# Two steps of a feed-forward at a time: elementwise instructions over pairs of tiles in double PSUM banks

## The chip, the cores and the metric

The kernel runs on one core of a Trainium2 chip (trn2). The metric is the device time of one execution in microseconds, and a kernel's number is the median of its runs. Five engines work side by side and wait for each other through semaphores: PE (TensorE, matrix products, with its weight loads PEld), DVE (VectorE), ACT (ScalarE), POOL (GpSimd) and SP, which issues the DMAs. Each engine takes its instructions strictly in the order in which they were written; an instruction that waits holds up everything behind it on its engine.

## What is computed

The input is `x`, four batches of 12416 tokens with 128 channels, and 32 inducing points. First comes an attention of the inducing points over the tokens, then one of the tokens over its result; the outcome goes, token by token, through a gated feed-forward with 1536 hidden channels:

```python
def mab(q, kv):
    s = scale * (q @ kv.transpose(0, 2, 1))
    s = s - s.max(-1, keepdims=True)
    a = np.exp(s)
    a /= a.sum(-1, keepdims=True) + 1e-09
    return a @ kv
h = mab(I, x)            # (4, 32, 128)
x = mab(x, h)            # (4 * 12416, 128)
g = x @ w_gate
out = (g * (1 / (1 + np.exp(-g))) * (x @ w_val)) @ w_out
```

All of it is float32. Products whose operands are split into a leading part and a rest (`hi` and `lo`, type fp32r) are summed so that the result keeps float32's accuracy.

## The kernel before

**Tiles and columns.** The tokens of a batch are cut into 25 columns of 512 or 480 tokens (`COLS`; in each batch 13 columns of 512, then 12 of 480). A column runs through 12 tiles (`NT`), one for each 128 hidden channels. One (column, tile) is a slot; a batch has 300 of them. The weights of the tokens' attention and of the gate and value projections are multiplied together beforehand (`st.w`, tile `tw`), so that a slot's gate and value are one product each of a stacked attention matrix (`stack`) with a piece of `tw`.

**A slot.** `front` (L680) issues the products g (L691) and v (L692), each into a single PSUM bank of the six of pool `ps_gv`. `gate` (L695) runs silu on ACT from g's bank into `silu` (two buffers). `value` (L699) multiplies v by it on DVE: into `h`, a pool of three buffers (`BF[1]`), or, for the tiles in `DVE_TILES` (1, 5 and 9), back into v's own PSUM bank. `split` (L707), called one slot later, makes `h_hi` by a cast on ACT (L713; on DVE for tile 11 and for slots with a burst, below) and `h_lo = h - h_hi` (L715) on POOL, or on DVE for `DVE_TILES`, whose h lies in PSUM. `back` (L719) adds three products into the bank o of the column: `wo_lo` by hi (L729), `wo_hi` by hi (L730), `wo_hi` by lo (L731). After tile 11 `evac` copies o out on DVE (L738) and SP stores it. The 12 slots of the very first column (`u.whole`) have a simpler form and lie in the start-up.

**The order of the work.** All instructions are written out by the loop at L769 to L794. In each slot it writes front, gate and value, then the split of the slot before, then steps of the attention of this batch and of the next one that are due (`plan`, `post`), then as many backs as keep no more than `ahead` slots between front and back. `ahead` is `SKEW` (5) as a rule, so the three products into o come five slots behind their g and v. Ahead of a burst it climbs by one in `RAMP` slots, up to `HI` (10), and falls back to `SKEW` at the burst: the stored backs are then written at once. A burst is a slot in which ACT runs exponentials of the next batch (`exp1_part` L302, `exp2` L456); there are two for each of the batches that follow, and one (`E0`) in the first. The attention's own products (L270, L318, L420) take banks of `ps_gv` and `ps_o`; on DVE its steps are copies, transposes and reductions of around 0.6 us, on POOL they are subtractions and products (L453, L467, L483).

**Buffers.** An instruction that writes a buffer waits until all who read its last content are done. For `h` these are the cast on ACT and the subtraction on POOL, three h-tiles back. For `h_hi` (11 buffers) and `h_lo` (10) it is the products into o.

Of the kernel before, what the change touches and what calls it, by code (L numbers as in the profile page):

```python
# [105 lines left out]
def induced_set_attention_then_swiglu(ctx: ExitStack, tc: tile.TileContext, xt, xn, ind, wgv, wo, out):  # L106
# [573 lines left out]
    def front(st, b, c, t):  # L680
# [11 lines left out]
        nc.tensor.matmul(out=u.v[:, :n], lhsT=st.w[:, wcol(1, t)], rhs=rhs, start=True, stop=True)  # L692
        return u

    def gate(u):  # L695
        u.s = sip.tile([P, WF], F32, name="silu")
        nc.scalar.activation(out=u.s[:, :u.n], in_=u.g[:, :u.n], func=AF.Silu)  # L697

    def value(u):  # L699
        n = u.n  # L700
        if u.whole:
            u.h = hip.tile([P, WB], F32, name="h_hi")[:, :WF]
        else:
            u.h = u.v if u.t in DVE_TILES else hp.tile([P, WF], F32, name="h")
        nc.vector.tensor_mul(out=u.h[:, :n], in0=u.v[:, :n], in1=u.s[:, :n])  # L705

    def split(u):  # L707
        if u.whole:
            return
        n = u.n  # L710
        u.hi = hip.tile([P, WB], F32R, name="h_hi")[:, u.at[1]:u.at[1] + WF]
        u.lo = lop.tile([P, WB], F32R, name="h_lo")[:, u.at[2]:u.at[2] + WF]
        (nc.vector.tensor_copy if u.cast_dve else nc.scalar.copy)(out=u.hi[:, :n], in_=u.h[:, :n])  # L713
        eng = nc.vector if u.t in DVE_TILES or u.last else nc.gpsimd
        eng.tensor_sub(out=u.lo[:, :n], in0=u.h[:, :n], in1=u.hi[:, :n].bitcast(F32))  # L715

    acc = {}

    def back(u):  # L719
# [4 lines left out]
        ws = slice(P * t, P * t + P)
        if u.whole:
            k = t % (WP // P)
            nc.tensor.matmul(out=o[:, :n], lhsT=pieces[f"o{t // (WP // P)}"].w[:, P * k:P * k + P], rhs=u.h[:, :n], start=(t == 0), stop=(t == NT - 1))  # L727
        else:
            nc.tensor.matmul(out=o[:, :n], lhsT=wo_lo[:, ws], rhs=u.hi[:, :n], start=(t == 0), stop=False)  # L729
            nc.tensor.matmul(out=o[:, :n], lhsT=wo_hi[:, ws], rhs=u.hi[:, :n], start=False, stop=False)  # L730
            nc.tensor.matmul(out=o[:, :n], lhsT=wo_hi[:, ws], rhs=u.lo[:, :n], start=False, stop=(t == NT - 1))  # L731
# [23 lines left out]
    ahead = len(pend)
    for b in range(B):
        nxt = attention(b + 1, (one, oneb)[(b + 1) % 2]) if b + 1 < B else None
        if nxt is not None:
            nxt.steps = plan(nxt, PA if b == 0 else PB)
            if b == 0:  # L760
                cur.steps.append((nxt.e1, lambda: run(f"e2:52:{NTB}")))
                for q in range(2, NF):
# [4 lines left out]
        bursts = (nxt.bursts if nxt is not None else set()) | ({E0} if b == 0 else set())
        last_burst = max(bursts, default=0)
        for slot in range(NT if b == 0 else 0, SLOTS):  # L769
            c, t = slot // NT, slot % NT  # L770
            u = front(cur, b, c, t)
            gate(u)
            value(u)
            u.cast_dve = t in CAST
            u.last = b == B - 1 and slot == SLOTS - 1
# [4 lines left out]
            if slot in bursts:  # L780
                u.cast_dve = True
                split(u)
                pend.append(wait.pop(0))
            for a in (cur, nxt):
                while a is not None and a.steps and a.steps[0][0] <= slot:

                    if pend and pend[0].t in getattr(a.steps[0][1], "acc", ()):
                        break
                    a.steps.pop(0)[1]()
            ahead = min(ahead + 1 / RAMP, HI) if nxt is not None and slot < last_burst else max(ahead - 1 / RAMP, SKEW)  # L790
            if slot in bursts:
                ahead = SKEW - (b == 0)
            while len(pend) + len(wait) > ahead:
                back(pend.pop(0))  # L794
# [44 lines left out]
```

## Time and profile before

| | |
|---|---|
| three runs | 1454.93 us median (1454.5 to 1455.03) |
| profiled execution, span of its instructions | 1453.1 us |
| PE busy | 1441.8 us, 99% |
| DVE, ACT, POOL busy | 1187.8, 1281.9, 1207.9 us (82%, 88%, 83%) |
| PE in two quiet stretches (1160 to 1260 us, 1300 to 1400 us) | 100.00 of 100 us in each |

The span is that of one profiled execution. Busy time of an engine is the time in which at least one of its instructions ran; neighbours overlap a little, so mean durations added up come to more than busy time. In a timeline row the first number is the start in us, the second the length, and a bracket at the end tells how long the engine had been idle and what ended that. In a group's row stand the count, the busy us, the mean ns of one, and the idle time before them.

### The profile page before, as it was taken

Reading aid. Unit: us, or ns where it says so; the run is one execution under the profiler, and the core shown is the slowest. Engines: PE = TensorE matmul, PEld = TensorE weight load, DVE = VectorE, ACT = ScalarE, POOL = GpSimd, SP = SyncE. Lnnn points to the kernel's source line nnn. Section 1 sums busy time; section 2 is a strip of 40 time slices with the busy share of each in tenths; the row PEclk is TensorE's granted clock in tenths of the full one; section 3 lists DMA queues with packets and bytes.
Section 4 is the critical chain, followed back from the end, with each engine's and each line's share of the span. In section 5 each row is a group of like instructions: output and inputs, shape, how many; then the busy total and the mean of one; then the engine's idle time right before and its main releaser. Section 6 shows DMA issues by size and latency. Waiting matters only on the chain.

```text
span 1453.1 us, 24926 instructions
## 1 busy us (share of the span) xinstructions
PE 1441.8 (99%) x7452; PEld 1173.5 (81%) x7452; DVE 1187.8 (82%) x2080; ACT 1281.9 (88%) x2388; POOL 1207.9 (83%) x995
## 2 busy tenths in 40 slices
PE   8999999999999999999999999999999999999999
PEld 5577788788887787888888778688888888888887
DVE  6888778887888788888788778988888878878877
ACT  5888898799998887999999888799999999999997
POOL 1689778888998778898899878879889889889987
PEclk9999999999999999999999999999999999999999
DMA  9233522321143242211123522321111111111110
GB/s 369 68 98 126 185 74 97 106 64 56 36 138 136 88 137 106 70 52 42 35 69 111 189 78 93 107 79 35 42 36 42 37 44 37 40 40 38 39 41 21
DMA packets 50822, 119.80 MB, mean 82 GB/s; under 512 B 11392, under 2 KB 28288, under 8 KB 50688
## 3 DMA queue, kind: packets, MB, share of 16 engines
q1 hardware_dynamic: 50688, 118.22, 24.9%
q8 instruction: 59, 0.97, 0.3%
q14 instruction: 75, 0.61, 0.1%
HBM read 62.87 MB, written 25.43 MB: 61 GB/s over the span
## 4 chain that ended last, share of the span: by engine, by line
PE 95%; DMA 2%; ACT 1%; POOL 1%; DVE 0%; SPq 0%; issue 0%; DVEq 0%; ACTq 0%; POOLq 0%
PE gv L691 18%; PE o L729 18%; PE gv L692 18%; PE o L730 18%; PE o L731 18%; PE gv L270 2%; PE o L318 1%; DMA s_all<-wgv 1%; DMA xt<-xt 1%; PE o L270 1%; PE o L727 1%; POOL h_lo L715 0%; ACT silu L697 0%; PE gv L420 0%; ACT h_hi L713 0%; PE gv L398 0%
## 5 line engine op out<-in xcount | busy, mean ns | idle before, releaser
L715 POOL TENSOR_TENSOR h_lo<-h,h_hi 128x512 fp32r<-128x512 f32 (+1 forms) x890 | 1110.9, 1273 | 198.4 <-ACT h_hi L713 140.4
L697 ACT ACTIVATE silu<-gv 128x512 f32<-128x512 f32 (+1 forms) x1200 | 704.7, 588 | 109.3 <-PE gv L691 76.3
L705 DVE TENSOR_TENSOR h<-gv,silu 128x512 f32<-128x512 f32 (+1 forms) x891 | 594.5, 668 | 199.0 <-ACT silu L697 147.7
L713 ACT CAST h_hi<-h 128x512 fp32r<-128x512 f32 (+1 forms) x788 | 474.7, 602 | 30.1 <-DVE h L705 25.3
L691 PE MATMUL gv<-stack,tw 128*128 128x512 f32 (+1 forms) x1200 | 465.9, 388 | 2.1 <-DVE stack L543 1.3
L692 PE MATMUL gv<-stack,tw 128*128 128x512 f32 (+1 forms) x1200 | 461.5, 385 | 0.7 <-ACT silu L697 0.4
L729 PE MATMUL o<-h_hi,wo_lo 128*128 128x512 f32 (+1 forms) x1188 | 458.4, 386 | 0.0
L730 PE MATMUL o<-h_hi,wo_hi 128*128 128x512 f32 (+1 forms) x1188 | 456.9, 385 | 0.0
L731 PE MATMUL o<-h_lo,wo_hi 128*128 128x512 f32 (+1 forms) x1188 | 456.3, 384 | 0.0
L691 PEld LDWEIGHTS gv<-stack,tw 128*128 128x128 f32 x1200 | 225.4, 188 | 50.5 <-ACT tw L412 2.6
L729 PEld LDWEIGHTS o<-h_hi,wo_lo 128*128 128x128 f32 x1188 | 223.0, 188 | 51.8 <-issue 12.1
L692 PEld LDWEIGHTS gv<-stack,tw 128*128 128x128 f32 x1200 | 224.9, 187 | 47.8 <-ACT silu L697 4.2
L731 PEld LDWEIGHTS o<-h_lo,wo_hi 128*128 128x128 f32 x1188 | 222.6, 187 | 40.5 <-POOL h_lo L715 0.4
L730 PEld LDWEIGHTS o<-h_hi,wo_hi 128*128 128x128 f32 x1188 | 223.1, 188 | 38.9
L705 DVE TENSOR_TENSOR gv<-gv,silu 128x512 f32<-128x512 f32 (+1 forms) x297 | 201.8, 680 | 40.2 <-ACT silu L697 39.1
L715 DVE TENSOR_TENSOR h_lo<-gv,h_hi 128x512 fp32r<-128x512 f32 (+1 forms) x297 | 197.3, 664 | 0.9
L713 ACT CAST h_hi<-gv 128x512 fp32r<-128x512 f32 (+1 forms) x294 | 167.5, 570 | 4.9 <-DVE gv L705 3.9
L738 DVE COPY ob<-o 128x512 f32<-128x512 f32 (+1 forms) x100 | 66.3, 663 | 0.8 <-PE o L731 0.8
L713 DVE CAST h_hi<-h 128x512 fp32r<-128x512 f32 (+1 forms) x103 | 52.0, 506 | 0.0
L483 POOL TENSOR_TENSOR a_lo<-aT,a_hi 128x480 fp32r<-128x480 f32 (+2 forms) x26 | 34.6, 1330 | 0.0
L190 POOL TENSOR_TENSOR wgv_sb<-s_all 128x512 int32<-128x512 int32 x2 | 2.9, 1455 | 28.9 <-ACT s_all L178 28.9
L467 POOL TENSOR_TENSOR s_all<-s_all,sm 128x512 f32<-128x512 f32 (+2 forms) x27 | 26.1, 967 | 0.0
(155 smaller groups left out, 476.2 us busy)
## 6 DMA issues: line engine op xcount, KB each, us to landing
xt_sb<-xt SPq DMA_DIRECT2D x32, 896.0 KB, 5.2
xn_sb<-xn SPq DMA_DIRECT2D x18, 896.0 KB, 5.6
out<-ob SPq DMA_DIRECT2D x52, 256.0 KB, 2.0
out<-ob SPq DMA_DIRECT2D x48, 240.0 KB, 2.0
stack<-a_hi SPq DMA_DIRECT2D x96, 64.0 KB, 2.0
stack<-a_lo SPq DMA_DIRECT2D x96, 64.0 KB, 2.0
stack<-a_hi SPq DMA_DIRECT2D x96, 60.0 KB, 2.0
stack<-a_lo SPq DMA_DIRECT2D x96, 60.0 KB, 2.0
```

The source lines that it names most:

```text
L270: nc.tensor.matmul(out=ps[32 * j:32 * j + 32, 32 * (lo - b0):32 * (hi - b0)], lhsT=lhsT, rhs=st.xt[q][:, lo - CH0[q]:hi - CH0[q], j, :], s ...
L483: eng.tensor_sub(out=st.al[q][:, :n], in0=st.at[q][:, :n], in1=st.ah[q][:, :n].bitcast(F32))
L691: nc.tensor.matmul(out=u.g[:, :n], lhsT=st.w[:, wcol(0, t)], rhs=rhs, start=True, stop=True)
L692: nc.tensor.matmul(out=u.v[:, :n], lhsT=st.w[:, wcol(1, t)], rhs=rhs, start=True, stop=True)
L697: nc.scalar.activation(out=u.s[:, :u.n], in_=u.g[:, :u.n], func=AF.Silu)
L705: nc.vector.tensor_mul(out=u.h[:, :n], in0=u.v[:, :n], in1=u.s[:, :n])
L713: (nc.vector.tensor_copy if u.cast_dve else nc.scalar.copy)(out=u.hi[:, :n], in_=u.h[:, :n])
L715: eng.tensor_sub(out=u.lo[:, :n], in0=u.h[:, :n], in1=u.hi[:, :n].bitcast(F32))
L729: nc.tensor.matmul(out=o[:, :n], lhsT=wo_lo[:, ws], rhs=u.hi[:, :n], start=(t == 0), stop=False)
L730: nc.tensor.matmul(out=o[:, :n], lhsT=wo_hi[:, ws], rhs=u.hi[:, :n], start=False, stop=False)
L731: nc.tensor.matmul(out=o[:, :n], lhsT=wo_hi[:, ws], rhs=u.lo[:, :n], start=False, stop=(t == NT - 1))
L738: nc.vector.tensor_copy(out=ob[:, :n], in_=o[:, :n])
```

## The change

Everything behind the start-up works on pairs of slots of one column: tiles 0 and 1, 2 and 3, and so on to 10 and 11.

- The six single banks become three double banks (`ps_two`, 2 x 512 columns each). `fronts` writes the products in the order g g v v, the g's into the halves of one double bank and the v's into those of another.
- Silu, the product with v, the cast and the subtraction each become one instruction over 2 x 512 (or 2 x 480) columns, except where the two tiles of a pair are on different engines (`both`): the subtraction of tiles 0 and 1, the cast of tiles 10 and 11. The last pair of the program is done in single halves.
- h always lies in SBUF. The pools in numbers of pairs (`BF`): silu 2, h 2, h_hi 6, h_lo 6. In single tiles they were 2, 3, 11, 10.
- `DVE_TILES` is 1, 4 and 5 in place of 1, 5 and 9. `HI` is 8 in place of 10, `SKEW` 6 in place of 5, counted in tiles; the backs of a pair come together, six products into o, three pairs behind their front.
- The attention's products that took a bank of `ps_gv` take a half of a double bank (`bank`).
- The build sets aside a smaller scratch area for DMA descriptors (`dynamic_dma_scratch_size=4096`).

```diff
-HI = 10
+HI = 8
-BF = (2, 3, 11, 10)
-SKEW = 5
+BF = (2, 2, 6, 6)
+SKEW = 6
-DVE_TILES = {1, 5, 9}
+DVE_TILES = {1, 4, 5}
...
+    def fronts(st, b, c, t):
+        us = []
+        g, v = two(), two()
...
+        for k, x in enumerate((g, v)):
+            for u in us:
+                nc.tensor.matmul(out=x[:, 512 * (u.t - t):][:, :u.n], lhsT=st.w[:, wcol(k, u.t)], rhs=st.stack[c][:, :u.n], start=True, stop=True)
...
+    def gates(u):
+        s = sip.tile([P, 2 * WF], F32, name="silu")
+        u.s = pair(s, u)
+        g = pair(u.g, u)
+        each(u, u.last, lambda f: nc.scalar.activation(out=f(u.s), in_=f(g), func=AF.Silu))
+
+    def values(u):
+        u.h = pair(hp.tile([P, 2 * WF], F32, name="h"), u)
+        v = pair(u.v, u)
+        each(u, u.last, lambda f: nc.vector.tensor_mul(out=f(u.h), in0=f(v), in1=f(u.s)))
 
     def split(u):
...
+        both([x.t in CAST or u.cast_dve for x in u.us], (nc.scalar.copy, nc.vector.tensor_copy), lambda e, f: e(out=f(u.hi), in_=f(u.h)))
+        both([x.t in DVE_TILES or (u.last and x is u) for x in u.us], (nc.gpsimd, nc.vector),
+             lambda e, f: e.tensor_sub(out=f(u.lo), in0=f(u.h), in1=f(u.hi.bitcast(F32))))
...
-        for slot in range(NT if b == 0 else 0, SLOTS):
-            c, t = slot // NT, slot % NT
-            u = front(cur, b, c, t)
-            gate(u)
-            value(u)
...
+        for slot2 in range(NT if b == 0 else 0, SLOTS, 2):
+            c, t = slot2 // NT, slot2 % NT
+            u = fronts(cur, b, c, t)
+            u.last = b == B - 1 and slot2 == SLOTS - 2
+            u.cast_dve = burst = slot2 in bursts or slot2 + 1 in bursts
+            gates(u)
+            values(u)
             if wait:
                 split(wait[0])
-                pend.append(wait.pop(0))
+                pend += wait.pop(0).us
...
+                while len(pend) + 2 * len(wait) > ahead + (slot == slot2):
+                    back(pend.pop(0))
```

How the rows of the engines change is shown at a column of 480 tokens. The numbers behind the names tell buffers apart; a name in the brackets is the engine whose semaphore the instruction waits for. First DVE in the kernel before: L705 is the product with silu (into `h`, or into `gv` for a tile of `DVE_TILES`), L715 the subtraction, L738 the copy of o.

```order
L705 TENSOR_TENSOR h_10648<-gv_10643,silu_10646 128x480 [waits PE_49,Activation_49,Pool_49]
L705 TENSOR_TENSOR h_10668<-gv_10663,silu_10666 128x480 [waits PE_49,Activation_49,Pool_49]
L738 COPY ob_10677<-o_10499 128x480 [waits DMAHW2_49,PE_49]
L705 TENSOR_TENSOR gv_10681<-gv_10681,silu_10684 128x480 [waits PE_49,Activation_49]
L705 TENSOR_TENSOR h_10701<-gv_10696,silu_10699 128x480 [waits PE_49,Activation_49,Pool_49]
L715 TENSOR_TENSOR h_lo_10704<-gv_10681,h_hi_10703 128x480 [waits Activation_49]
L705 TENSOR_TENSOR h_10716<-gv_10711,silu_10714 128x480 [waits PE_49,Activation_49,Pool_49]
L705 TENSOR_TENSOR h_10731<-gv_10726,silu_10729 128x480 [waits PE_49,Activation_49,Pool_49]
L705 TENSOR_TENSOR gv_10741<-gv_10741,silu_10744 128x480 [waits PE_49,Activation_49]
```

Then DVE in the changed kernel, over a column and the end of the one before: L755 is the product with silu, L768 the cast of tile 11, L770 the subtraction, L795 the copy of o. The first three rows are the products of the last two pairs of a column (tiles 8 and 9, then 10 and 11) and of the first pair of the next; the fourth is the cast of tile 11.

```order
L755 TENSOR_TENSOR h_7485<-gw_7478,silu_7483 128x2x480 [waits DVE_49,PE_49,Activation_49]
L755 TENSOR_TENSOR h_7505<-gw_7498,silu_7503 128x2x480 [waits PE_49,Activation_49,Pool_49]
L755 TENSOR_TENSOR h_7525<-gw_7518,silu_7523 128x2x480 [waits PE_49,Activation_49,Pool_49]
L768 CAST h_hi_7527<-h_7505 128x480 [waits DVE_49]
L755 TENSOR_TENSOR h_7546<-gw_7539,silu_7544 128x2x480 [waits PE_49,Activation_49,Pool_49]
L770 TENSOR_TENSOR h_lo_7549<-h_7525,h_hi_7548 128x480 [waits Activation_49]
L755 TENSOR_TENSOR h_7572<-gw_7565,silu_7570 128x2x480 [waits PE_49,DVE_49,Activation_49,Pool_49]
L795 COPY ob_7584<-o_7470 128x480 [waits DMAHW7_49,PE_49]
L755 TENSOR_TENSOR h_7595<-gw_7588,silu_7593 128x2x480 [waits PE_49,Activation_49,Pool_49]
L770 TENSOR_TENSOR h_lo_7598<-h_7572,h_hi_7597 128x2x480 [waits Activation_49]
```

Every product now writes an h in SBUF and waits for the subtraction that read the h two pairs before; where that ran on POOL, the wait is for POOL. In the order before, that wait was for the h-tile three back. The cast of tile 11 stands behind the product of the next column's first pair.

POOL at the same places, first before, six h-tiles in a row:

```order
L715 TENSOR_TENSOR h_lo_10651<-h_10633,h_hi_10650 128x480
L715 TENSOR_TENSOR h_lo_10671<-h_10648,h_hi_10670 128x480
L715 TENSOR_TENSOR h_lo_10688<-h_10668,h_hi_10687 128x480
L715 TENSOR_TENSOR h_lo_10719<-h_10701,h_hi_10718 128x480
L715 TENSOR_TENSOR h_lo_10734<-h_10716,h_hi_10733 128x480
L715 TENSOR_TENSOR h_lo_10748<-h_10731,h_hi_10747 128x480
```

and in the changed kernel, from tiles 6 and 7 of one column (first row) over 8 and 9, 10 and 11, tile 0 alone, 2 and 3, to tiles 6 and 7 of the next (last row):

```order
L770 TENSOR_TENSOR h_lo_7488<-h_7464,h_hi_7487 128x2x480
L770 TENSOR_TENSOR h_lo_7508<-h_7485,h_hi_7507 128x2x480
L770 TENSOR_TENSOR h_lo_7528<-h_7505,h_hi_7527 128x2x480
L770 TENSOR_TENSOR h_lo_7549<-h_7525,h_hi_7548 128x480
L770 TENSOR_TENSOR h_lo_7575<-h_7546,h_hi_7574 128x2x480
L770 TENSOR_TENSOR h_lo_7619<-h_7595,h_hi_7618 128x2x480
```

Nine single subtractions of a column have become four of double length and one single; those of tiles 4 and 5 and of tile 1 are on DVE.

More of the change, by code (lines that the diff above doesn't have):

```diff
@@ L117, in induced_set_attention_then_swiglu, with two, bank @@
     oneb = ctx.enter_context(tc.tile_pool(name="oneb", bufs=1))
-    ps_gv = ctx.enter_context(tc.tile_pool(name="ps_gv", bufs=6, space=bass.MemoryType.PSUM))
     ps_o = ctx.enter_context(tc.tile_pool(name="ps_o", bufs=2, space=bass.MemoryType.PSUM))
+    single = ExitStack()
+    ps_gv = single.enter_context(tc.tile_pool(name="ps_gv", bufs=6, space=bass.MemoryType.PSUM))
+    ps_two = None
+    spare = []
+    def two():
+        del spare[:]
+        return ps_two.tile([P, 2 * 512], F32, name="gw")
+    def bank(second=0):
+        if ps_two is None:
+            return ps_gv.tile([P, 512], F32, name="gv")
+        if second and spare:
+            return spare.pop()
+        t = two()
+        spare.append(t[:, 512:])
+        return t[:, :512]
     pad = sgl.tile([P, 32], F32, name="pad")
@@ L218, in psum @@
             if xn0 is not None or second:
-                return ps_gv.tile([P, 512], F32, name="gv")
+                return bank(second)
             return ps_o.tile([P, 512], F32, name="o")
@@ L328, in h_a @@
         def h_a():
-            ps = ps_gv.tile([P, 512], F32, name="gv")
+            ps = bank()
             ns = NXN + 1
@@ L416, in proj_round @@
             weights()
-            ps = ps_gv.tile([P, 512], F32, name="gv")
+            ps = bank(i)
             for j in range(NG):
@@ L693, in front, with pair @@
         return u
+    def pair(x, u, off=0):
+        return x.rearrange("p (k w) -> p k w", k=2)[:, :, off:off + u.n]
     def gate(u):
-        u.s = sip.tile([P, WF], F32, name="silu")
+        u.s = sip.tile([P, 2 * WF], F32, name="silu")[:, :WF]
         nc.scalar.activation(out=u.s[:, :u.n], in_=u.g[:, :u.n], func=AF.Silu)
     def value(u):
-        n = u.n
-        if u.whole:
-            u.h = hip.tile([P, WB], F32, name="h_hi")[:, :WF]
-        else:
-            u.h = u.v if u.t in DVE_TILES else hp.tile([P, WF], F32, name="h")
@@ L705, in value @@
-        nc.vector.tensor_mul(out=u.h[:, :n], in0=u.v[:, :n], in1=u.s[:, :n])
-    def split(u):
[L708 to L715, printed above, removed]
+        u.h = hip.tile([P, 2 * WB], F32, name="h_hi")[:, :WF]
@@ new lines, in each @@
+    def each(u, last, call):
+        if last:
+            for k in range(2):
+                call(lambda x: x[:, k])
+        else:
+            call(lambda x: x)
+    def gates(u):
[7 more added lines that the diff above has]
+        each(u, u.last, lambda f: nc.vector.tensor_mul(out=f(u.h), in0=f(v), in1=f(u.s)))
@@ new lines, in split, with both @@
+    def split(u):
+        u.hi = pair(hip.tile([P, 2 * WB], F32R, name="h_hi"), u, u.at[1])
+        u.lo = pair(lop.tile([P, 2 * WB], F32R, name="h_lo"), u, u.at[2])
+        def both(on, eng, call):
+            if u.last or on[0] != on[1]:
+                for k in range(2):
+                    call(eng[on[k]], lambda x: x[:, k])
+            else:
+                call(eng[on[0]], lambda x: x)
+        both([x.t in CAST or u.cast_dve for x in u.us], (nc.scalar.copy, nc.vector.tensor_copy), lambda e, f: e(out=f(u.hi), in_=f(u.h)))
+        both([x.t in DVE_TILES or (u.last and x is u) for x in u.us], (nc.gpsimd, nc.vector),
+             lambda e, f: e.tensor_sub(out=f(u.lo), in0=f(u.h), in1=f(u.hi.bitcast(F32))))
+        for k, x in enumerate(u.us):
+            x.hi, x.lo = u.hi[:, k], u.lo[:, k]
@@ L768, in induced_set_attention_then_swiglu @@
         last_burst = max(bursts, default=0)
-        for slot in range(NT if b == 0 else 0, SLOTS):
-            c, t = slot // NT, slot % NT
-            u = front(cur, b, c, t)
-            gate(u)
-            value(u)
-            u.cast_dve = t in CAST
-            u.last = b == B - 1 and slot == SLOTS - 1
+        for slot2 in range(NT if b == 0 else 0, SLOTS, 2):
[5 more added lines that the diff above has]
+            values(u)
             if wait:
                 split(wait[0])
-                pend.append(wait.pop(0))
+                pend += wait.pop(0).us
             wait.append(u)
-            if slot in bursts:
-                u.cast_dve = True
+            if burst:
                 split(u)
[L783 to L794, printed above, removed]
+                pend += wait.pop(0).us
+            for slot in (slot2, slot2 + 1):
+                for a in (cur, nxt):
+                    while a is not None and a.steps and a.steps[0][0] <= slot:
+                        if pend and pend[0].t in getattr(a.steps[0][1], "acc", ()):
+                            break
+                        a.steps.pop(0)[1]()
+                ahead = min(ahead + 1 / RAMP, HI) if nxt is not None and slot < last_burst else max(ahead - 1 / RAMP, SKEW)
+                if slot in bursts:
+                    ahead = SKEW - (b == 0)
+                while len(pend) + 2 * len(wait) > ahead + (slot == slot2):
+                    back(pend.pop(0))
         if nxt is not None:
@@ L799, in induced_set_attention_then_swiglu @@
         split(u)
-    for u in pend + wait:
+        pend += u.us
+    for u in pend:
         back(u)
```

19 lines of the change are left out of this document (15 added, 4 removed).

## Prediction

> **What bounds the kernel now.** I read the page first (busy times, the chain that ended last), then the stretches of two quiet windows, then the groups by line with shapes kept apart, then who waited for whom on DVE.
>
> ```profile
> span 1453.1 us, 24926 instructions
> PE 1441.8 (99%) x7452; PEld 1173.5 (81%) x7452; DVE 1187.8 (82%) x2080; ACT 1281.9 (88%) x2388; POOL 1207.9 (83%) x995
> PE 95%; DMA 2%; ACT 1%; POOL 1%; DVE 0%; SPq 0%; issue 0%; DVEq 0%; ACTq 0%; POOLq 0%
> ...
> 1160.00:1260.00 100.00, 100.00 (x443) 82.78 (x442) 81.27 (x134) 92.61 (x170) 88.42 (x71) 1.00 0.13 41
> 1300.00:1400.00 100.00, 100.00 (x465) 86.80 (x464) 81.18 (x142) 92.20 (x178) 88.42 (x74) 1.00 0.13 38
> ...
> L729 PE MATMUL o<-h_hi,wo_lo 128*128 128x512 f32 x612 | 240.9, 394 | 0.0
> L729 PE MATMUL o<-h_hi,wo_lo 128*128 128x480 f32 x576 | 217.6, 378 | 0.0
> ```
>
> In the window rows stand the length, then busy time and count of PE, PEld, DVE, ACT and POOL, then the granted clock. PE is never idle there: 443 products in 100 us are 0.2257 us each at 512 columns, 465 are 0.2151 us at 480. A column of 12 tiles has 60 products, so it takes 13.54 or 12.90 us. The two L729 rows count the columns (one of its products per tile): 612/12 = 51 of 512 and 576/12 = 48 of 480. The clock is full (1.00). So PE is the bound, and whatever the change saves elsewhere is worth nothing by itself: the products stay 60 per column. The most that a better order could gain is PE's idle time, 1453.1 - 1441.8 = 11.3 us. For g g v v and six of o I book zero: each product still loads its own weights, and the loads (82.78 of 100 us) run beside the products.
>
> So the question is whether the other four engines still keep PE fed. Before, they have room, but one wait already shows how h's buffers work:
>
> ```profile
> DVE h L705 <- POOL h_lo L715: 15.6, 32, 0.9
> ```
>
> The product with silu waited 32 times, at most 0.9 us, for a subtraction on POOL: that of the h three h-tiles back. The change makes this wait longer on both sides: the instructions are twice as long, and there are two buffers in place of three.
>
> **The durations.** The singles, and for POOL a shape that it has at two lengths:
>
> ```profile
> L705 DVE TENSOR_TENSOR h<-gv,silu 128x512 f32<-128x512 f32 x459 | 312.9, 683 | 100.1 <-ACT silu L697 67.0 <-POOL h_lo L715 9.9 <-issue 6.6
> L705 DVE TENSOR_TENSOR h<-gv,silu 128x480 f32<-128x480 f32 x432 | 281.6, 652 | 98.9 <-ACT silu L697 80.7 <-POOL h_lo L715 5.6 <-PE gv L691 3.4
> L713 ACT CAST h_hi<-h 128x512 fp32r<-128x512 f32 x405 | 249.8, 617 | 20.9 <-DVE h L705 17.4
> L713 ACT CAST h_hi<-h 128x480 fp32r<-128x480 f32 x383 | 224.9, 587 | 9.2 <-DVE h L705 7.9
> L715 POOL TENSOR_TENSOR h_lo<-h,h_hi 128x512 fp32r<-128x512 f32 x459 | 590.7, 1312 | 121.3 <-ACT h_hi L713 85.1 <-PE o L730 17.2 <-DVE h_hi L713 9.8
> L715 POOL TENSOR_TENSOR h_lo<-h,h_hi 128x480 fp32r<-128x480 f32 x431 | 520.5, 1233 | 77.1 <-ACT h_hi L713 55.3 <-DVE h_hi L713 13.9 <-PE o L731 3.9
> L467 POOL TENSOR_TENSOR s_all<-s_all,sm 128x512 f32<-128x512 f32 x12 | 12.9, 1076 | 0.0
> L467 POOL TENSOR_TENSOR s_all<-s_all,sm 128x128 f32<-128x128 f32 x3 | 1.2, 409 | 0.0
> ...
> 341.74 0.66 DVE L705 TENSOR_TENSOR h<-gv,silu 128x480 f32<-128x480 f32 x1 [0.38 <-ACT silu L697]
> 342.31 0.40 DVE L713 CAST h_hi<-h 128x480 fp32r<-128x480 f32 x1
> ...
> 1441.67 0.58 ACT L713 CAST h_hi<-h 128x480 fp32r<-128x480 f32 x1
> 1442.34 1.23 POOL L715 TENSOR_TENSOR h_lo<-h,h_hi 128x480 fp32r<-128x480 f32 x1 [0.71 <-ACT h_hi L713]
> ```
>
> *Product M.* 512 against 480 columns gives (683 - 652)/32 = 0.97 ns per column; a double one is 683 + 512 x 0.97 = 1.18 us, at 480 it is 1.12 us. *Cast C on ACT*, in the same way: 0.94 ns per column, 1.10 and 1.04 us. *Cast of tile 11 on DVE*: 0.40 us, starting 0.09 us before the product ahead of it ends. *Subtraction S on POOL*: no row shows a double one. Upper end: twice the single, 2.62 and 2.47 us. Lower end: the second half at L467's rate, (1076 - 409)/384 = 1.74 ns per column, though L467 reads a smaller second operand: 2.20 and 2.07 us. I take the single twice less the fixed part that L467 shows, 409 - 128 x 1.74 = 187 ns: 2.44 and 2.28 us, since dispatch is what one instruction in place of two saves. The Trainium skill, page "GPSIMD Engine Reference", section "Elementwise — side-by-side cycle accounting", has 4497 ns for such an operation on 2048 columns; half of that is an estimate of 2.25 us at 1024, and the sum below would come out some 70 us lower by it. *Hand-over* from ACT to POOL: 1442.34 - (1441.67 + 0.58) = 0.09 us; for the others I take 0.05 as the mean between nothing and this.
>
> **The sum: a ring around the h buffers.** Call the pairs of a column A (tiles 0, 1) to F (10, 11). By the rows of the change, M of a pair waits for the subtraction two pairs back, and POOL takes D, E, F, tile 0, B. Follow it from the end of D's subtraction in one column to the same point in the next: POOL does E (S); the next column's A needs E's h buffer (M); the cast of tile 11 stands behind it on DVE (0.40); F's subtraction needs this cast (S); B's product needs F's buffer (M); B is cast (C) and subtracted (S); D's product needs B's buffer (M); D is cast (C) and subtracted (S). Nothing in this ring can overlap: 4 S + 3 M + 2 C + 0.40 + 8 x 0.05 - 0.09.
>
> At 512 columns: 9.76 + 3.54 + 2.20 + 0.71 = 16.21 us against PE's 13.54. At 480: 9.12 + 3.36 + 2.08 + 0.71 = 15.27 against 12.90. The ring takes PE's place as the bound. It costs 51 x 2.67 + 48 x 2.37 = 250 us. With the ends of S: 161 us (2.20 and 2.07) to 323 us (2.62 and 2.47).
>
> The other parts:
>
> *Attention's products.* They no longer lengthen the span where PE idles anyway.
>
> ```profile
> by line: PE gv L691 18.1%; PE o L729 18.1%; PE gv L692 18.1%; PE o L730 18.0%; PE o L731 17.8%; PE gv L270 1.9%; PE o L318 1.2%; DMA s_all<-wgv 1.0%; DMA xt<-xt 0.8%; PE o L270 0.7%; PE o L727 0.7%; POOL h_lo L715 0.4%; ACT silu L697 0.4%;
> ...
> 508.87 2.53 PE o L318 x84
> ```
>
> L270 and L318 are 3.8% of 1453, 55 us, in lumps up to 2.53 us, about what a column now leaves idle. Between 0 and -55; I take -45.
>
> *Bursts.* ACT does nothing for the feed-forward from 503.25 to 509.68:
>
> ```profile
> 503.25 1.28 ACT L302 ACT_TABLE_LOAD   x1
> ...
> 509.68 0.60 ACT L697 ACTIVATE silu<-gv 128x512 f32<-128x512 f32 x1
> ```
>
> That is 6.4 us. Stored backs covered it: HI - SKEW = 5 tiles of three products, 5 x 3 x 0.2257 = 3.4 us, plus three slots in six single banks. Now 8 - 6 = 2 tiles are 1.4 us, and the next v but one waits for a bank that only the next silu frees. The cost of one is 2.0 us (the lost backs alone) to 6.4 (the ring stands still); I take 4, since the burst's own pair is cast on DVE. Seven bursts: +28 (14 to 45).
>
> *Attention on DVE and POOL* runs mostly in the ring's gaps (DVE idles while the ring is on POOL): +10 (0 to 25).
>
> *Without price:* silu, two buffers (its product is two pairs old when needed, and the ring spaces them over 4.7 us); three double banks (a front waits for the product two pairs back, which in the ring is done 1.6 us ahead); the attention's halves (evacuated within a pair); the lag of three pairs; the last pair in halves; the scratch area. If one of these covers were gone, 0.3 to 0.8 us at its place.
>
> 1453.1 + 250 - 45 + 28 + 10 = 1696 us of span. The median of the runs lies 1.8 us above the profiled span (1454.93 against 1453.1): 1698 us.
>
> **The rivals.** *(1) PE stays the bound, and the kernel is not slower.* The place is POOL's double subtraction; the ring fits into PE's column if S is at most (13.54 - 6.45)/4 = 1.77 us, at 480 (12.90 - 6.15)/4 = 1.69. For it: one dispatch less. Against it: its second half would have to run at 0.9 ns per column, where POOL's cheapest row has 1.74. It would give 1455 less part of the 11.3 us: 1450 us. Chance 0.03. *(2) A cheap subtraction, below L467's rate but above that point*, say 2.00 and 1.88 us: the ring is 1.76 and 1.60 us shorter, 250 - 167 = 83 us; less idle PE absorbs some 25: 1455 + 83 - 25 + 28 + 10 = 1551 us. Chance 0.10. *(3) DVE loses the port to POOL.* Before, this cast took 2.70 us in place of 0.40:
>
> ```profile
> 587.12 2.70 DVE L713 CAST h_hi<-h 128x512 fp32r<-128x512 f32 x1
> ...
> 586.42 0.96 POOL L453 TENSOR_TENSOR s_all<-s_all,mx2a 128x448 f32<-128x448 f32 x1
> 587.32 1.31 POOL L715 TENSOR_TENSOR h_lo<-h,h_hi 128x512 fp32r<-128x512 f32 x1
> 588.56 0.96 POOL L453 TENSOR_TENSOR s_all<-s_all,mx2b 128x448 f32<-128x448 f32 x1
> ```
>
> It ended 0.3 us after three POOL instructions in a row (588.56 + 0.96 = 589.52). The Trainium skill, page "SBUF — State Buffer", section "Who interferes with whom", calls it an exclusive lock, taken also by a DVE instruction with two SBUF inputs; this trace agrees for the cast. By it the subtractions on DVE, whose h now lies in SBUF, can wait in the same way. In the ring's quiet columns POOL is idle when they come, and behind E it has nothing but F, which needs the cast. If in half the columns something of the attention stood there, 2.3 us x 50 = 115 us more: 1813 us. Chance 0.07.
>
> **How the numbers follow.** Forecast 0.80 at 1698 us. Its low end is the lower S without bursts: 1455 + 161 - 45 + 10 = 1581, its high end the upper S: 1455 + 323 - 45 + 28 + 10 = 1771. The range 1580 to 1775 leaves out rivals 1 and 2 below and 3 above, 0.20. A difference of 0.2% is about what a measurement of this kernel can tell from none. Only rival 1 is not slower: faster 0.02, within 0.2% 0.01, slower 0.97.
>
> **What would show it.** In the changed profile: PE busy down to around 85%, with gaps of 2 to 3 us per column; columns of around 16.2 and 15.3 us in the quiet stretches; in the waits, DVE's product (L755) for POOL's subtraction (L770) at the top with several hundred us; POOL's double subtraction at 2.44 and 2.28 us; POOL idle behind E for M and the cast. It is wrong if PE stays near 99%, if L755 hardly waits for POOL, or if PE waits at bursts alone.

## The result and the profile after

| | before | after |
|---|---|---|
| median of the runs | 1454.91 us (1454.5 to 1455.03, 4 runs) | 1807.12 us (1805.1 to 1810.01, 4 runs) |
| ratio to before | | 1.2422, 95% interval 1.2404 to 1.2439 |
| span of the profiled execution | 1453.1 us | 1806.2 us |

The change costs 24%. The direction of the forecast was right, but the time lies 109 us above the 1698 forecast and 32 us above the range's upper end. The page of the changed kernel: span, busy time, and the chain that ended last, by engine and by line.

```profile
span 1806.2 us, 21321 instructions
...
PE 1590.0 (88%) x7452; PEld 1157.6 (64%) x7452; DVE 1144.6 (63%) x1385; ACT 1188.8 (66%) x1300; POOL 1146.1 (63%) x600
...
POOL 33%; PE 25%; DVE 22%; ACT 12%; issue 6%; DMA 1%; POOLq 0%; SPq 0%; DVEq 0%; ACTq 0%
POOL h_lo L770 33%; DVE h L755 16%; PE gw L734 10%; ACT h_hi L768 8%; PE o L786 4%; PE o L788 4%; PE o L787 4%; DVE h_hi L768 3%; ACT silu L750 2%; PE gw L286 2%; DVE h_lo L770 1%; PE o L334 1%; DMA s_all<-wgv 1%; DMA xt<-xt 1%; DVE s_all L457 0%
```

No engine is the bound by its load: POOL, DVE and ACT are each busy for less time than before, and PE has gone from 99% to 88%. The chain says what it is: two thirds of it lie on POOL, DVE and ACT (33, 22 and 12%), where 95% lay on PE before. The waits of the changed kernel (sum in us, times, longest) name two places:

```profile
DVE h L755 <- POOL h_lo L770: 508.3, 344, 2.7
...
PE gw L286 <- DVE s_all L457: 29.6, 8, 5.8
...
PE gw L436 <- DVE eT L439: 18.3, 3, 7.2
...
PE gw L286 <- DVE s_all L296: 12.6, 6, 2.2
```

**The ring.** DVE's product waits 344 times for POOL's subtraction, against 32 times before. One quiet column in the timeline of the changed kernel (start, length, and in brackets the idle time before), POOL first:

```profile
1651.30 2.28 POOL L770 TENSOR_TENSOR h_lo<-h,h_hi 128x960 fp32r<-128x960 f32 x1 [1.13 <-ACT h_hi L768]
1655.88 4.68 POOL L770 TENSOR_TENSOR h_lo<-h,h_hi 128x960 fp32r<-128x960 f32 x2 [2.31 <-ACT h_hi L768]
1662.24 3.41 POOL L770 TENSOR_TENSOR h_lo<-h,h_hi 128x960 fp32r<-128x960 f32 x2 [1.68 <-DVE h_hi L768]
```

And DVE:

```profile
1649.03 1.16 DVE L755 TENSOR_TENSOR h<-gw,silu 128x960 f32<-128x960 f32 x1 [2.44 <-POOL h_lo L770]
...
1653.61 1.16 DVE L755 TENSOR_TENSOR h<-gw,silu 128x960 f32<-128x960 f32 x1 [1.00 <-POOL h_lo L770]
...
1660.59 1.16 DVE L755 TENSOR_TENSOR h<-gw,silu 128x960 f32<-128x960 f32 x1 [1.25 <-POOL h_lo L770]
1661.67 0.40 DVE L768 CAST h_hi<-h 128x480 fp32r<-128x480 f32 x1
1664.51 1.16 DVE L755 TENSOR_TENSOR h<-gw,silu 128x960 f32<-128x960 f32 x1 [2.44 <-POOL h_lo L770]
```

Read it in order of time: product of B at 1649.03, its subtraction from 1651.30 to 1653.58, product of D at once (1653.61), D and E subtracted until 1660.56, product of the next A (1660.59), the cast of tile 11 behind it (1661.67), F's subtraction from 1662.24, product of the next B at 1664.51. This is the ring of the prediction, step for step; POOL stands idle three times in it although it is what everybody waits for. It took 1664.51 - 1649.03 = 15.48 us, where 15.27 was forecast.

**The columns with attention.** I cut the trace into columns at the first `wo_lo` product of each. Of the 99, 34 lie in the three stretches in which attention runs on PE (columns 0 to 15, 27 to 35, 52 to 60); 65 are quiet. The quiet ones grew by 173.7 us (forecast 21 x 2.67 + 44 x 2.37 = 160.4). The 34 grew by 178.4 us, from 528.5 to 706.9, where the forecast comes to 30 x 2.67 + 4 x 2.37 - 45 + 28 + 10 = 82.6. So 96 of the 109 us that are missing lie there. The window rows of one such stretch (columns 27 to 35) and of ten quiet columns of 480 (87 to 96). Before:

```profile
454.90:596.30 141.40, 141.36 (x860) 108.29 (x859) 117.84 (x209) 117.85 (x209) 110.29 (x90) 1.00 0.35 118
1296.40:1426.00 129.60, 129.60 (x601) 112.49 (x601) 104.70 (x181) 119.80 (x231) 112.99 (x95) 1.00 0.12 37
```

After:

```profile
563.30:756.30 193.00, 159.08 (x866) 112.32 (x866) 120.29 (x152) 112.17 (x118) 107.74 (x57) 0.93 0.26 87
1619.90:1775.40 155.50, 142.91 (x602) 108.10 (x602) 98.48 (x111) 109.97 (x122) 106.71 (x54) 1.00 0.10 31
```

The nine columns with attention went from 141.4 to 193.0 us, 5.7 each, and the granted clock (third number from the right) is 0.93 in them; the ten quiet ones went from 129.6 to 155.5, 2.6 each, at a full clock. What happens in the nine, at the longest wait, in PE's timeline:

```profile
737.85 0.85 PE L436 MATMUL gw<-wgv_sb,hT 128*32 128x384 f32 x8 [0.21 <-DVE h L755]
745.88 1.51 PE L436 MATMUL gw<-wgv_sb,hT 128*32 128x384 f32 x8 [7.18 <-DVE eT L439]
747.32 0.80 PE L786 MATMUL o<-h_hi,wo_lo 128*128 128x512 f32 x1
747.91 0.63 PE L787 MATMUL o<-h_hi,wo_hi 128*128 128x512 f32 x1
748.34 0.63 PE L788 MATMUL o<-h_lo,wo_hi 128*128 128x512 f32 x1
748.77 0.60 PE L786 MATMUL o<-h_hi,wo_lo 128*128 128x512 f32 x1
```

Meanwhile on DVE:

```profile
739.82 1.23 DVE L755 TENSOR_TENSOR h<-gw,silu 128x1024 f32<-128x1024 f32 x1 [2.03 <-POOL h_lo L770]
740.96 1.02 DVE L768 CAST h_hi<-h 128x512 fp32r<-128x512 f32 x2
742.01 2.75 DVE L770 TENSOR_TENSOR h_lo<-h,h_hi 128x512 fp32r<-128x512 f32 x1
744.69 0.54 DVE L438 CAST eT<-gw 128x384 fp32r<-128x384 f32 x1
745.27 0.56 DVE L439 TENSOR_TENSOR eT<-gw,eT 128x384 fp32r<-128x384 f32 x1
```

Eight products of the attention go into the first half of a double bank. The eight for its second half wait 7.18 us until DVE has read the first (L438, L439), since the two halves are one tile and a write into it waits for its reader. DVE is not late because of those reads (1.1 us): they stand in its queue behind a product that waits for POOL, two casts, and a subtraction that took 2.75 us. Behind the wait the products come 0.43 us apart (747.91, 748.34, 748.77), where they were 0.23 before it; the granted clock from 745.8 to 749.0 is 0.50.

### The profile page after: what moved, and what is told of

Same layout as the page of the kernel before. It is cut to its first block, busy times and chain, and to the rows that moved or that the text cites. A ratio compares the mean times of both kernels' runs of the same rounds, so it can differ in the third digit from the quotient of the medians.

```text
span 1806.2 us, 21321 instructions
## 1 busy us (share of the span) xinstructions
PE 1590.0 (88%) x7452; PEld 1157.6 (64%) x7452; DVE 1144.6 (63%) x1385; ACT 1188.8 (66%) x1300; POOL 1146.1 (63%) x600
## 4 chain that ended last, share of the span: by engine, by line
POOL 33%; PE 25%; DVE 22%; ACT 12%; issue 6%; DMA 1%; POOLq 0%; SPq 0%; DVEq 0%; ACTq 0%
POOL h_lo L770 33%; DVE h L755 16%; PE gw L734 10%; ACT h_hi L768 8%; PE o L786 4%; PE o L788 4%; PE o L787 4%; DVE h_hi L768 3%; ACT silu L750 2%; PE gw L286 2%; DVE h_lo L770 1%; PE o L334 1%; DMA s_all<-wgv 1%; DMA xt<-xt 1%; DVE s_all L457 0%
## 5 line engine op out<-in xcount | busy, mean ns | idle before, releaser
L770 POOL TENSOR_TENSOR h_lo<-h,h_hi 128x1024 fp32r<-128x1024 f32 (+3 forms) x495 | 1050.9, 2131 | 608.7 <-ACT h_hi L768 429.3
L755 DVE TENSOR_TENSOR h<-gw,silu 128x1024 f32<-128x1024 f32 (+1 forms) x595 | 705.4, 1186 | 608.7 <-POOL h_lo L770 508.3
L768 ACT CAST h_hi<-h 128x1024 fp32r<-128x1024 f32 (+3 forms) x587 | 560.6, 955 | 384.3 <-DVE h L755 381.1
L734 PE MATMUL gw<-stack,tw 128*128 128x512 f32 (+1 forms) x2376 | 671.5, 404 | 48.7 <-DVE h L755 36.9
L750 ACT ACTIVATE silu<-gw 128x1024 f32<-128x1024 f32 (+1 forms) x595 | 591.5, 995 | 183.5 <-PE gw L734 177.1
L734 PEld LDWEIGHTS gw<-stack,tw 128*128 128x128 f32 x2376 | 420.5, 189 | 243.0 <-DVE h L755 170.5
L770 DVE TENSOR_TENSOR h_lo<-h,h_hi 128x512 fp32r<-128x512 f32 (+1 forms) x199 | 199.7, 1003 | 0.2
L795 DVE COPY ob<-o 128x512 f32<-128x512 f32 (+1 forms) x100 | 66.3, 663 | 0.7 <-PE o L788 0.7
L286 PE MATMUL gw<-xt_sb,hTs 128*32 128x448 f32 (+5 forms) x184 | 25.4, 659 | 33.9 <-DVE s_all L457 29.6
L768 DVE CAST h_hi<-h 128x480 fp32r<-128x480 f32 (+2 forms) x103 | 52.9, 516 | 0.2
L334 PE MATMUL o<-xn_sb,eT 128*32 128x128 f32 x582 | 23.7, 324 | 7.1 <-DVE eT L324 4.9
L286 PE MATMUL gw<-xt_sb,indT 128*32 128x448 f32 (+1 forms) x120 | 15.7, 618 | 13.5 <-DVE s_all L296 12.6
```

Source lines behind the costliest of these rows:

```text
L286: nc.tensor.matmul(out=ps[32 * j:32 * j + 32, 32 * (lo - b0):32 * (hi - b0)], lhsT=lhsT, rhs=st.xt[q][:, lo - CH0[q]:hi - CH0[q], j, :], s ...
L334: nc.tensor.matmul(out=st.hps[32 * g:32 * g + 32, 0:C], lhsT=st.eT[q][:, 32 * i:32 * i + 32], rhs=st.xn[q][:, i, :], start=(tb < NG), stop ...
L734: nc.tensor.matmul(out=x[:, 512 * (u.t - t):][:, :u.n], lhsT=st.w[:, wcol(k, u.t)], rhs=st.stack[c][:, :u.n], start=True, stop=True)
L750: each(u, u.last, lambda f: nc.scalar.activation(out=f(u.s), in_=f(g), func=AF.Silu))
L755: each(u, u.last, lambda f: nc.vector.tensor_mul(out=f(u.h), in0=f(v), in1=f(u.s)))
L768: both([x.t in CAST or u.cast_dve for x in u.us], (nc.scalar.copy, nc.vector.tensor_copy), lambda e, f: e(out=f(u.hi), in_=f(u.h)))
```

## The experiments

Two theories of the whole. **Ring and halves:** the two buffers of h close the ring, which sets the quiet columns; the wait at the second half adds itself in the attention's columns. **Rivals:** POOL's (or PE's) load sets the columns, whatever h's buffers are; and the attention's columns are long because of bursts or of the attention's own work. Each run has its own median of the kernel before beside it (1454.9 to 1455.5 us). Stretch and quiet columns are those of the window rows above.

| run | median, us | ratio to before (95%) | columns 27 to 35 | columns 87 to 96 |
|---|---|---|---|---|
| after | 1807.12 | 1.2422 (1.2404 to 1.2439) | 193.0 | 155.5 |
| e1_h3 | 1584.07 | 1.088 (1.0861 to 1.0898) | 169.7 | 134.6 |
| e2_halves | 1738.9 | 1.1943 (1.1925 to 1.1961) | 173.7 | 155.5 |
| e3_cast_act | 1678.53 | 1.1535 (1.1515 to 1.1554) | 183.1 | 141.2 |
| e4_sub_e_dve | 1800.05 | 1.2367 (1.2348 to 1.2385) | 191.3 | 154.3 |
| e5_h3_halves | 1536.95 | 1.0559 (1.0543 to 1.0575) | 156.5 | 134.5 |
| e6_sub_a_dve | 1529.53 | 1.0508 (1.049 to 1.0525) | 152.6 | 134.9 |
| e7_hi10 | 1528.87 | 1.0504 (1.0489 to 1.052) | 149.4 | 134.6 |
| e8_h3_halves_cast | 1531.25 | 1.052 (1.0504 to 1.0535) | 157.3 | 133.1 |
| e9_cast_hi10 | 1511.77 | 1.0386 (1.0369 to 1.0404) | 146.1 | 133.0 |
| e10_skew8 | 1518.79 | 1.0447 (1.0425 to 1.0469) | 152.3 | 131.9 |
| e11_skew8_a_dve | 1505.49 | 1.0352 (1.0336 to 1.0367) | 151.2 | 131.7 |
| e12_hi12 | 1509.78 | 1.0379 (1.0365 to 1.0393) | 148.4 | 131.8 |

**Three buffers for h.**

```diff
-BF = (2, 2, 6, 6)
+BF = (2, 3, 5, 6)
```

> Edit: h, the double products, gets three buffers, and h_hi gives one up (five). Ring theory (POOL's subtraction must end before DVE may write the next product into the same one of h's two buffers): with three buffers the subtraction waited for lies one pair further back, the ring opens, and the quiet columns fall from 16.4 / 15.5 us (512 / 480 columns) to 13.6 to 13.9 / 13.0, near PE's own 60 products; what the attention's columns lose stays: 1535 to 1570 us in all, and the wait of DVE's product on POOL's subtraction falls from 508 us to under 100. Rival (POOL's own load, or the lag of PE behind the cast, sets the columns, and h's buffers only show it): quiet columns stay at 16 to 16.5 / 15.2 to 15.6, and the time at 1780 to 1810 us.

It took 1584.07 us: one more buffer takes 223 of the 352 us away. The wait at the top of the list is nearly gone:

```profile
DVE h L755 <- POOL h_lo L770: 5.7, 3, 2.3
```

The ten quiet columns come close to before's 129.6, while the stretch with attention keeps most of its length (windows of this run):

```profile
500.40:670.10 169.70, 149.72 (x866) 112.04 (x865) 126.39 (x152) 111.15 (x118) 112.36 (x57) 0.96 0.29 99
1420.40:1555.00 134.60, 132.43 (x602) 111.85 (x601) 106.06 (x111) 107.44 (x121) 110.68 (x55) 1.00 0.12 36
```

POOL is busy for 1195.0 us in this run and for 1146.1 in the kernel after the change, so its load is not what set the columns. The time is 14 us above the expected span. The attention's columns still have their waits, and the subtractions on DVE have grown (groups by form, L770 on DVE; count, busy us, mean ns). The kernel after the change:

```profile
L770 DVE TENSOR_TENSOR h_lo<-h,h_hi 128x512 fp32r<-128x512 f32 x51 | 48.4, 949 | 0.1
L770 DVE TENSOR_TENSOR h_lo<-h,h_hi 128x480 fp32r<-128x480 f32 x49 | 33.6, 685 | 0.0
```

And this run:

```profile
L770 DVE TENSOR_TENSOR h_lo<-h,h_hi 128x512 fp32r<-128x512 f32 x51 | 78.9, 1546 | 0.1
...
L770 DVE TENSOR_TENSOR h_lo<-h,h_hi 128x480 fp32r<-128x480 f32 x49 | 73.6, 1502 | 0.0
```

In the kernel after the change 45 of the 49 at 480 columns ran while POOL was idle, or nearly so (0.65 us); here every one of the 49 ran beside work on POOL and took 1.50 us on the mean: what rival 3 feared, in the kernel where the ring doesn't cover it.

**Both halves before either is read.**

```diff
+    held = []
+    def evacuate(call):
+        if spare:
+            held.append(call)
+        else:
+            flush()
+            call()
...
-            ev(out=hi, in_=ps[:, :PC])
+            def out():
+                ...
+            evacuate(out)
```

> Edit: the attention's products into both halves of a double PSUM bank are issued before DVE reads either half; the feed-forward is unchanged. Theory of the halves (PE waits at the second half until DVE, which stands in the ring, has read the first): quiet columns unchanged at 16.4 / 15.5 us, PE's waits at L286 and L436 on DVE's reads of the first half vanish, the columns with attention lose 3 to 8 us each where such a wait stood, 60 to 100 us in all, so 1710 to 1745 us. Rival (the attention's columns are long because of bursts, of the clock or of the attention's own load on DVE and POOL, and the wait at the half only takes the place of another): under 20 us gained, 1787 us or more.

It took 1738.9 us, 68 less than the change as it stands. The 34 columns lose 66.6 us (640.3 in place of 706.9); the quiet ones stay (1032.4 and 1033.1). The same place as above, with the 16 products of both halves in one piece (L450 is L436 before the edit):

```profile
695.67 1.50 PE L450 MATMUL gw<-wgv_sb,hT 128*32 128x384 f32 x16 [0.17 <-DVE h L772]
...
704.91 1.16 PE L751 MATMUL gw<-stack,tw 128*128 128x512 f32 x4 [3.22 <-DVE eT L454]
```

The window row of the stretch:

```profile
536.10:709.80 173.70, 154.15 (x866) 111.45 (x865) 119.83 (x152) 112.72 (x118) 109.66 (x57) 0.97 0.28 96
```

The wait of 7.18 us is gone; one of 3.22 us comes later, when the next front needs the bank that DVE is still reading. So the halves carry 67 of the 96 us, at the place where the prediction had booked nothing. Not all of it is waiting: PE's three waits at second halves listed above sum to 60.5 us, and with them most of the slow products went. In both traces the granted clock is either 1.00 or 0.50; PE was busy at 0.50 for 72 us in the 34 columns of the kernel after the change, and for 28 us in these.

**Tile 11 cast on ACT.**

```diff
-CAST = {11}
+CAST = set()
```

> Edit: tile 11 is no longer cast on DVE by itself; ACT casts tiles 10 and 11 with one double instruction, so that in the ring DVE's next product comes 0.4 us earlier and F's subtraction waits for ACT instead. Ring theory: the step by DVE's cast goes out of the way from E to F, ACT's cast of F has been waiting on nothing else, and with one product and one cast less in the ring the column is 14.4 / 13.5 us: about 190 us less, near 1620 us. Rival (POOL's or PE's load sets the column): no change within 10 us.

1678.53 us, 129 less. That is 58 us above the 1620 expected. The quiet columns have a median of 14.62 and 13.80 us, where 14.4 and 13.5 were expected, and ten of the 44 at 480 tokens stay at 15.3 to 15.4: the way by DVE's cast is a link of the ring, as the theory has it, but the ring without it is longer than I worked out, and is still closed (`DVE h L755` waits 393.2 us for POOL). Why these ten stay long was not followed. The rival's "no change" is out: POOL's and PE's work is the same here.

**E's subtraction on DVE.**

```diff
-DVE_TILES = {1, 4, 5}
+DVE_TILES = {1, 4, 5, 8, 9}
```

> Edit: the subtraction of pair E (tiles 8 and 9) goes from POOL to DVE, which takes a fifth of POOL's load away and puts 1.2 us on DVE inside the ring. Ring theory: DVE's subtraction takes the place of POOL's between the two ends of the ring; the column is 16.0 / 15.1 us, 0.3 to 0.4 less than now, and the time 1770 to 1810 us. Rival (POOL's load as such sets the column: 4 to 5 double subtractions of 2.4 us and what the attention adds): 2 us or more off each column, 1700 us or less.

1800.05 us, 7 less, inside the ring theory's range; quiet columns 16.32 and 15.43, which is 0.05 to 0.07 less where 0.3 to 0.4 were expected. The page's row of POOL's work:

```profile
L770 POOL TENSOR_TENSOR h_lo<-h,h_hi 128x1024 fp32r<-128x1024 f32 (+3 forms) x396 | 819.5, 2080 | 825.4 <-ACT h_hi L768 396.3
```

POOL was busy 1146.1 us and is now busy 918.0 (51%), and almost nothing came of it. Next to the two runs above this settles the first question: what counts is where an instruction stands in the ring, not how much POOL has to do.

**Both remedies together.** e5 joins the edits of e1 and e2.

> Edit: three buffers for h (h_hi five) and the attention's products into both halves issued before DVE reads either, together. Theory (the ring around h's buffers and the wait at the halves are two causes, and nothing else of size is left): quiet columns as with three buffers alone, 13.9 / 13.2 us; the attention's 34 columns lose what the halves took alone, 60 to 70 us; 1505 to 1530 us. Rival (the two hide one another: with the ring open DVE comes in time for the first half anyway, and the halves are worth little): 1560 to 1585 us, like three buffers alone.

1536.95 us, 47 below three buffers alone, where 60 to 70 were expected: with the ring open DVE comes earlier to the first half, and the halves are worth less (the same three waits sum to 45.5 us in e1's trace, against 60.5). The rival's "little" is wrong too: in columns 27 to 35 they take 13 of 170 us.

**What is left.** Seven more runs look for the rest. Four change one thing of e5 each, or join two:

```diff
e6:
-DVE_TILES = {1, 4, 5}
+DVE_TILES = {0, 1, 4, 5}
e7:
-HI = 8
+HI = 10
e8:
-CAST = {11}
+CAST = set()
e9 (e7 and e8):
+HI = 10
+CAST = set()
```

> Edit: as the run with three buffers and both halves, and tile 0's subtraction goes from POOL to DVE, so that pair A is subtracted by DVE with one double instruction. Theory (what is left in the quiet columns is the third POOL subtraction in a row, E, F and tile 0, for whose result PE waits where the attention or a lock loss comes on top): the columns of 14.4 us become 13.3, the others fall by 0.1 to 0.2 us, 10 to 25 us in all. Rival (DVE's subtraction of two SBUF operands, now twice as long, loses to POOL more often): 0 to 30 us slower than the run that it is made from.

> Edit: as the run with three buffers and both halves, and ten tiles of stored backs ahead of a burst in place of eight (what the kernel before has). Burst theory (the backlog that the change gave up is missed at each of seven bursts): two more tiles of three products at 0.2257 us are 1.35 us per burst, so 6 to 10 us faster. Rival (at the bursts ACT and the PSUM banks set the time, and stored backs only move it): within 3 us.

> Edit: as the run with three buffers and both halves, and tile 11 is cast on ACT with tile 10 in one double instruction. Theory (with three buffers the ring is open, so DVE's cast is not on the path that sets the end; it costs DVE 0.4 us, and a lock loss now and then): within 10 us of the run that it is made from. Rival (the ring still bounds): 30 us or more faster.

> Edit: the two small gains together on the run with three buffers and both halves: tile 11 cast on ACT with tile 10, and ten tiles of stored backs ahead of a burst. Theory (the one took 0.2 to 0.3 us from each quiet column, the other 10 us from the attention's columns, at different places): they add, 1520 to 1525 us. Rival (the cast on ACT makes ACT late behind a burst, and eats what the stored backs give): 1528 to 1533 us.

e6: 1529.53 us, 7 faster where 10 to 25 were expected, and not at the place named: the columns of 14.4 us stayed at 14.4, so that reason fell. e7: 1528.87 us, 8 faster, inside the 6 to 10 that two stored tiles at seven bursts come to. e8: 1531.25, 6 faster, as expected; its ordinary quiet columns are 13.00 and 13.60 us, before's 12.96 and 13.60. e9: 1511.77, 25 under e5, which is more than the sum of both (14) and below what theory and rival had; why was not found.

```diff
e10 (on e9):
-SKEW = 6
+SKEW = 8
e11 (on e10):
+DVE_TILES = {0, 1, 4, 5}
e12 (on e11):
-BF = (2, 3, 5, 6)
-HI = 10
+BF = (2, 3, 6, 5)
+HI = 12
```

> Edit: as the run with both small gains, and PE's products of o lag eight tiles behind in place of six. Theory (one quiet column in four or five is 1.5 to 2 us long because the attention's last steps on POOL make a subtraction late and PE waits 1.4 us for it; another pair of lag is 2.2 us of cover): these columns come down to 13.0 / 13.6 us like the rest, some 16 of them, 20 to 35 us in all, 1490 to 1505 us. Rival (POOL is short of time over those columns as a whole, and the lag only moves the wait): within 5 us.

> Edit: as the run with a lag of eight tiles, and tile 0's subtraction on DVE with tile 1's. Theory (POOL's row of three subtractions is still what comes late in the attention's columns): 3 to 10 us faster than with the lag alone. Rival (with the lag PE no longer waits for POOL, and DVE's longer subtraction costs locks): 0 to 10 us slower.

> Edit: as the last and fastest run so far (three buffers, both halves, tile 11 cast on ACT, a lag of eight tiles, pair A subtracted on DVE), with twelve tiles of backs ahead of a burst in place of ten, and h_hi six, h_lo five buffers. Burst theory (what counts is the stock, the tiles ahead less the lag: two before this edit, four after; a stock of four in place of two took 11 us off the attention's columns once, and giving the two up by the longer lag cost 10): 8 to 11 us faster, 1494 to 1498 us. Rival (with one h_lo buffer less POOL and DVE stop where the stock is full, or the gain hung on the lag of six): within 4 us, 1501 us or more. Either way it stays slower than the kernel before by 2.5 to 3.5%.

e10: 1518.79, 7 slower, and its theory fell for the most part. The columns of 14.5 us (480 tokens) did become 13.0, but their neighbours went from 13.0 to 13.3 and 13.6, so the 65 quiet columns gained 6 us in place of 20 to 35: the lag seems only to move POOL's lateness on. The 34 columns lost 10 us, while the stock ahead of a burst (`HI` less `SKEW`) went from four tiles to two. e11: 1505.49, 13 faster (3 to 10 expected), the best of all. e12: 1509.78, no gain, much as the rival had it; POOL now stops for its buffers of `h_lo`, which e11's trace does not show:

```profile
POOL h_lo L787 <- PE o L805: 23.7, 9, 4.9
```

So the stock is worth 8 us where it was tried alone (e7), and e12 leaves open whether two more tiles would be worth as much with enough buffers. The page of e11, the best version:

```profile
span 1507.0 us, 20998 instructions
...
PE 1464.0 (97%) x7452; PEld 1177.2 (78%) x7452; DVE 1205.0 (80%) x1289; ACT 1208.8 (80%) x1301; POOL 1037.5 (69%) x501
```

PE is the bound again, and the version is still 3.5% slower than the kernel before (1.0336 to 1.0367). No run here beats the kernel before.

## Why the prediction was wrong in size

**The bound: right.** PE fell from 99% to 88% busy (forecast around 85%), and L755 on L770 leads the waits with 508 us.

**Durations: right.** The changed kernel's rows for the four double instructions:

```profile
L770 POOL TENSOR_TENSOR h_lo<-h,h_hi 128x1024 fp32r<-128x1024 f32 x204 | 493.9, 2422 | 354.9 <-ACT h_hi L768 246.3 <-DVE h_hi L768 95.9 <-DVE negmax L314 10.8
L770 POOL TENSOR_TENSOR h_lo<-h,h_hi 128x960 fp32r<-128x960 f32 x191 | 432.6, 2265 | 226.9 <-ACT h_hi L768 156.1 <-DVE h_hi L768 64.6 <-PE gw L734 2.0
L755 DVE TENSOR_TENSOR h<-gw,silu 128x1024 f32<-128x1024 f32 x306 | 373.1, 1220 | 337.5 <-POOL h_lo L770 258.8 <-ACT silu L750 49.0 <-ACT h_hi L768 6.2
L768 ACT CAST h_hi<-h 128x1024 fp32r<-128x1024 f32 x251 | 263.0, 1048 | 183.7 <-DVE h L755 181.2 <-POOL h_lo L770 1.4
```

S is 2.42 and 2.27 us (taken: 2.44 and 2.28), M 1.22 (1.18), C 1.05 (1.10); in the ring these small errors nearly cancel. The estimate by the Trainium skill's page "GPSIMD Engine Reference", section "Elementwise — side-by-side cycle accounting", was 2.25 at 1024 columns; the trace has 2.42, so its sum, 70 us lower, would have been further off. Rival 2 needed 2.00 and is out, rival 1 with it.

**The ring: right.** Quiet columns have a median of 16.39 and 15.48 us (16.21 and 15.27 forecast). Of the 0.2 us that are over, 0.12 is one hand-over: F's subtraction starts 0.17 us behind DVE's cast (1662.24 against 1661.67 + 0.40), where 0.05 was taken. All that the 65 quiet columns are over comes to 13 us. e1 opens the ring at its buffers; e3 and e4, which change a link each, bear it out too, though with columns 0.2 to 0.3 us longer than worked out.

**"The attention's halves (evacuated within a pair)", without price: this step failed.** The prediction listed them among the covers whose loss would cost "0.3 to 0.8 us at its place". The cover is that DVE reads the first half soon. But in the ring DVE's queue stands still for 2.0 to 2.4 us at a time, and the reads wait behind that: up to 7.2 us at a place, 60.5 us at 17 places. At the price put down they would have been 5 to 14 us. Taking the wait away gave back 67 us (e2). The profile of before could have told it: the prediction's own ring says that DVE's products wait for POOL, and the attention's reads are written into the same queue. I priced what the ring does to the feed-forward, and treated DVE as free for the rest ("runs mostly in the ring's gaps").

**Attention absorbed, bursts, attention's load (-45, +28, +10): too low by about 29.** With the halves out of the way the 34 columns are still 640.3 - 528.5 = 111.8 us longer, of which the ring accounts for 30 x 2.67 + 4 x 2.37 = 89.6. The three terms together were -7, and came to +22. How that divides was not separated. For one thing, nothing of the attention was absorbed on balance: against nine quiet columns of 512 tokens (13.60 us each before, 16.40 in e2), columns 27 to 35 are 19 us longer before and 26 in e2. The PE idle time that was to absorb the attention's products is partly spent on waits for banks (3.22 us in the rows of e2), so the -45 is the likelier part. For another, the sum took the clock as full throughout: the 28 us of PE work at the clock of 0.50 in these columns of e2 are up to 14 us lost, by an estimate that takes PE as the bound there. For the bursts, two tiles of stock are worth 8 us in all (e7), so the three tiles lost are some 12 by proportion, an estimate from another kernel.

**Rival 3 (DVE loses to POOL): in part.** Not in the quiet columns, as argued. In the attention's columns it is a piece of the halves' wait (2.75 us at 512 columns, where the mean is 0.95), and in e1 it lengthens these subtractions; how much of e1's time that is was not measured.

## What to carry to other kernels

When instructions are made twice as long, count the buffers between two engines in instructions, not in bytes: h went from three singles to two doubles, which is more room, yet the writer now waits for the reader two instructions back, and one more buffer was worth 223 us. When two banks become one tile, each reader of the one half stands between the writer and the other half: write both, then read. And a wait that is forecast for a queue holds up everything else in that queue, so price the others in it too. Longer elementwise instructions gained nothing here, where PE was the bound: DVE, ACT and POOL all became less busy by the change, and the best of the versions with them is still 3.5% slower.

## What was not expected of the hardware

- A subtraction on DVE with both operands in SBUF takes 0.65 us at 480 columns when POOL is idle (45 of the 49 after the change; the mean of all 49 is 0.69) and 1.50 us on the mean when POOL has a row of subtractions (e1). Before the change the same subtraction read h from PSUM and took 0.65 us at 480 columns, though POOL was at work beside nearly every one. POOL pays too: its single one goes from 1.24 to 1.64 us at 480 columns. POOL's group in the kernel after the change:

```profile
L770 POOL TENSOR_TENSOR h_lo<-h,h_hi 128x480 fp32r<-128x480 f32 x49 | 60.6, 1236 | 14.8 <-ACT h_hi L768 14.8
```

The same group in e1:

```profile
L770 POOL TENSOR_TENSOR h_lo<-h,h_hi 128x480 fp32r<-128x480 f32 x49 | 80.2, 1637 | 10.0 <-ACT h_hi L768 10.0
```

DVE's subtraction in the kernel before, from PSUM (gv):

```profile
L715 DVE TENSOR_TENSOR h_lo<-gv,h_hi 128x480 fp32r<-128x480 f32 x144 | 93.2, 647 | 0.1
```

- After PE waits of some us the products come slower for a while: 0.43 us apart behind the wait of 7.18 us and, in e2, behind the one of 3.22 us, at a granted clock of 0.50 and 0.51 (745.8 to 749.0, and 706.3 to 708.5 in e2). Over columns 27 to 35 the clock is 0.93, with 0.97 in e2, where the longer wait is gone, and 1.00 before. So a wait of PE can cost more than its own length: the 3.2 us at half clock behind the longer one are some 1.6 us of lost work, an estimate from these figures.
